# A planned order and split copies from two PSUM banks, in a kernel of banded attention and a maxout layer on one core

## The chip, the cores and the metric

The kernel runs on one core of a Trainium2 chip. The metric is the time of one execution on the device in microseconds (us). Engines: PE multiplies matrices (its weight loads are listed as PEld), DVE, ACT and POOL work elementwise, SP issues most transfers. All of them take their instructions in the order in which they are given and wait for one another by semaphores.

## The reference

Attention over 4 batches of 8 heads, 768 positions of 64 values, in which a query sees the 95 keys before it, itself, and the first 8 keys of its batch, with a bias that falls linearly with the distance; then a layer that takes the elementwise maximum of three products and multiplies it by an output matrix.

```python
    scores = scale * np.matmul(q, k.transpose(0, 1, 3, 2))
    is_global = pos[None, :] < int(n_global)
    is_local = (rel >= 0) & (rel < int(n_local))
    scores = scores + bias[None, :, :, :]
    scores = np.where(keep, scores, -1000000000.0)
    ...
    a = a / (np.sum(a, axis=-1, keepdims=True) + 1e-09)
    return np.matmul(a, v).astype(np.float32)
...
    h = np.maximum(np.maximum(x @ w1, x @ w2), x @ w3)
    return (h @ w_out).astype(np.float32)
```

x is the attention's output as 3072 rows of 512; w1, w2 and w3 are 512 by 768, w_out is 768 by 512.

## The kernel before

The 3072 rows are 24 tiles of 128, six to a batch. The second layer takes them in seven chunks of 4, 2, 2, 4, 4, 4 and 4 tiles. There is no loop over the work: a string, `SCHEDULE`, lists 494 units, and the program emits them one after the other. So the string is the order on every engine and in the SP queue. A unit is a letter and numbers; where a last number chooses an engine, 0 is ACT, 1 DVE and 2 POOL. The units:

- `l n.s`: load part s of group n of q and k (line 152, SP). The groups are 2, 2, 2, 6 and 6 tiles: tiles 0 to 17. `c n.s.how` casts it to bf16 (line 179), `x n.s.how` transposes it on PE into a PSUM tile and copies that to `qkT` (line 227). In the groups of 2 a part is all of q or all of k; in those of 6 a part is one pair of heads, 0 to 3 of q and 4 to 7 of k.
- `L`, `C`, `X`: the same for one tile (18 to 23). `X T.4` transposes by a DMA from SP (line 250). `C T.1.how` casts v of tile T; in `C T.how`, 3 means q on DVE and k on POOL (lines 195 to 197). `v T` loads v (line 170).
- `S T.g.how`: scores of tile T, four of its heads, against itself and the tile before, then the exponential on ACT (lines 268 to 289). With how 1 the bias is added by two matmuls (line 275); else `M T.g` multiplies by a mask on DVE (line 302). `K` and `B` prepare masks and bias.
- `G` and `V` carry the 8 global keys and values along (lines 210 and 219).
- `A T.how`: probabilities times v, then the normalisation on DVE (line 311: reciprocal, L331, and product, L332), which gives xb. `T T.how` transposes it into the chunk's `xT`: with 4 by a DMA from SP, else on PE with a copy (line 335).
- `F c.f.j`: product j of 3 for column block f of 6 of chunk c (line 355): four matmuls, then a copy on ACT (j = 0) or a maximum on DVE (j = 1, 2). `O c.t.how`: output product of one tile, six matmuls, a copy and a store from SP (line 385). `E` does the last chunk's four tiles (line 390).
- `w`, `o`: loads of the weights; `W g.j.how`, `Q i.how` cast them.

PSUM: `sp0` and `sp1` hold one S or A each; `psH` has three banks for F, O and some transposes; `psT` has one bank for transposes. A tile that is allocated from a full pool waits until the oldest is read. Loads of q and k rotate through six buffers (`raw`), casts through five, outputs through four (`ost`).

Of the kernel before, what the change touches and what calls it, by code (L numbers as in the profile page):

```python
# [13 lines left out]
BF16 = mybir.dt.bfloat16  # L14
# [44 lines left out]


# [1 line left out]
def kernel(  # L62
# [13 lines left out]
    nc = tc.nc  # L76
# [58 lines left out]
    raw, rawv, qb, qkT, Pt, xb = {}, {}, {}, {}, {}, {}  # L135
# [41 lines left out]
    copies = (nc.scalar.copy, nc.vector.tensor_copy, nc.gpsimd.tensor_copy)  # L177
# [49 lines left out]
    def u_x(n, s, how):  # L227
        bb, t0, sz, a, j0, jn = part(n, s)
        dst = batch_T(bb)[:, a, j0:j0 + jn, t0 * 128:(t0 + sz) * 128].rearrange("c j (i e) -> c j i e", e=sz)
        pool, tag = (psH, "h") if how in (2, 3, 5) else (psT, "tp")  # L230
        tp = pool.tile([128, sz, jn, 128], BF16, name="tpp", tag=tag)
        for e in range(sz):
            for j in range(jn):
                nc.tensor.transpose(tp[:, e, j],  # L234
                                    qb["p", n, s][:, e, 2 * j:2 * j + 2].rearrange("i h d -> i (h d)"), identb)

        src = tp.rearrange("c e j i -> c j i e")
        if how >= 4 and jn > 1:
            m = jn // 2
            nc.scalar.copy(dst[:, 0:m], src[:, 0:m])  # L240
            nc.vector.tensor_copy(dst[:, m:jn], src[:, m:jn])
# [196 lines left out]
    with tc.manual_schedule():  # L438
# [9 lines left out]
        for tvar in va_ring + va_first:  # L448
# [61 lines left out]
```

## Time and profile before

| | us |
|---|---|
| median of 4 runs (lowest to highest) | 182.62 (181.99 to 182.69) |
| the profiled execution's own time | 182.59 |
| its span, first to last instruction of the profile | 180.8 |
| HBM read and written | 25.17 MB and 6.29 MB, 174 GB/s over the span |
| first matmul (x0.0) | starts at 6.10 |
| first matmul of F0.0.0 | starts at 23.34 |
| last matmul | ends at 177.1 |
| last copy (ACT, L382) | starts at 177.75 |

The profile lists busy time of each engine and its share of the span; in the lists of waits each line names who waited, for whom, the total, the number of times and the longest. In the chain of waits each row is a start, a length and the work that set the end there, and "issue" is time in which nothing was waited for. A row of a timeline is a start, a length, the engine, the line and the operation with its tiles.

### The profile page before, as it was taken

What the parts mean: (1) busy time and instruction counts of PE and PEld (TensorE: products, weight loads), DVE (VectorE), ACT (ScalarE), POOL (GpSimd) and SP (SyncE); (2) the same over time, 40 slices, a digit from 0 to 9 for tenths busy, and PEclk for the clock granted to TensorE, in tenths of its full rate; (3) what the DMA queues carried; (4) which work ended last, traced back from release to release, by engine and by line L of the source; (5) the groups of instructions that cost most, each with busy time, mean ns of one, the idle gap of its engine ahead of it and who ended that gap; (6) DMA issues with size and microseconds to landing.
All of it is one profiled execution on the core that took longest, in us unless ns stands there. A gap on an engine that the chain in (4) does not pass through costs nothing.

```text
span 180.8 us, 3992 instructions
## 1 busy us (share of the span) xinstructions
PE 167.2 (92%) x1530; PEld 95.7 (53%) x1550; DVE 123.0 (68%) x233; ACT 108.3 (60%) x165; POOL 35.7 (20%) x68
## 2 busy tenths in 40 slices
PE   0499899999999999999999999999999999999991
PEld 0356644556876667865454554544455554444451
DVE  4457858788999988887798753966596474444610
ACT  5987987766699798595774398281717412212131
POOL 6775343223521303201130020010000000000000
PEclk9999999999999999999999999999999999999999
DMA  5999998999997899689999999996702440023015
GB/s 148 271 271 259 345 318 281 384 373 339 374 241 213 246 333 240 121 177 220 192 141 116 243 245 218 185 238 136 142 0 87 180 85 0 0 96 141 0 44 188
DMA packets 70819, 35.39 MB, mean 196 GB/s; under 512 B 53392, under 2 KB 65552, under 8 KB 70800
## 3 DMA queue, kind: packets, MB, share of 16 engines
q1 hardware_dynamic: 70656, 35.07, 79.3%
q8 instruction: 12, 0.20, 0.5%
q14 instruction: 7, 0.06, 0.1%
q10 hardware_dynamic: 144, 0.07, 0.1%
HBM read 25.17 MB, written 6.29 MB: 174 GB/s over the span
## 4 chain that ended last, share of the span: by engine, by line
PE 83%; DMA 7%; DVE 3%; SPq 2%; ACT 2%; issue 1%; ACTq 0%
PE h L361 48%; PE po L376 15%; PE sp L283 7%; PE tpp L234 4%; DMA rawp<-in_k_dram 3%; PE op L322 3%; DMA raw<-in_k_dram 3%; PE op L325 2%; PE sp L275 1%; DMA out_dram<-ost 1%; SPq L168 1%; ACT P L288 1%; PE xtp L349 1%; DVE xb L332 1%; SPq L175 1%
## 5 line engine op out<-in xcount | busy, mean ns | idle before, releaser
L361 PE MATMUL h<-xT,w 128*128 128x512 bf16 (+1 forms) x490 | 99.5, 348 | 0.8
L361 PEld LDWEIGHTS <-w 128*128 128x128 bf16 x504 | 46.9, 98 | 41.1 <-issue 0.7
L288 ACT ACTIVATE P<-sp 128x1024 bf16<-128x1024 f32 (+1 forms) x48 | 43.6, 954 | 16.7 <-PE sp L283 14.7
L366 ACT CAST h<-h 128x512 bf16<-128x512 f32 (+1 forms) x42 | 21.8, 530 | 28.7 <-PE h L361 28.2
L370 DVE TENSOR_TENSOR ht<-h,h 128x512 bf16<-128x512 bf16 (+1 forms) x42 | 25.4, 609 | 13.5 <-PE h L361 12.3
L376 PE MATMUL po<-wo,ht 128*128 128x512 bf16 (+2 forms) x150 | 33.3, 362 | 0.4
L368 DVE TENSOR_TENSOR h<-h,h 128x512 bf16<-128x512 bf16 (+1 forms) x42 | 25.1, 608 | 10.5 <-PE h L361 9.1
L307 DVE TENSOR_TENSOR P<-P,wmask 128x1024 bf16<-128x1024 bf16 x36 | 24.1, 696 | 3.2 <-ACT P L288 3.1
L376 PEld LDWEIGHTS <-ht 128*128 128x128 bf16 x156 | 14.1, 98 | 14.4
L382 ACT COPY ost<-po 128x512 f32<-128x512 f32 (+2 forms) x18 | 9.9, 558 | 17.7 <-PE po L376 14.4
L234 PE MATMUL tpp<-identb,qkp 128*128 128x128 bf16 x144 | 12.6, 240 | 6.5 <-POOL qkp L184 6.1
L332 DVE TENSOR_TENSOR xb<-op,rz 128x512 bf16<-128x512 f32 x24 | 16.6, 692 | 0.8
L283 PE MATMUL sp<-qkT 64*128 64x128 bf16 x352 | 15.5, 223 | 0.9 <-ACT qkT L240 0.7
L283 PEld LDWEIGHTS <-qkT 64*128 64x128 bf16 x352 | 10.2, 96 | 10.9 <-issue 7.8
L322 PEld LDWEIGHTS <-P 128*128 128x128 bf16 x192 | 12.7, 99 | 3.4 <-DVE P L309 0.9
L234 PEld LDWEIGHTS <-qkp 128*128 128x128 bf16 x144 | 10.1, 108 | 7.9 <-POOL qkp L184 6.3
L184 POOL CAST qkp<-rawp 128x768 bf16<-128x768 f32 (+1 forms) x11 | 10.1, 922 | 18.1 <-DMA rawp<-in_q_dram 11.7
L322 PE MATMUL op<-va,P 128*128 128x65 bf16 x160 | 12.7, 195 | 0.2 <-ACT P L288 0.2
L222 POOL COPY va<-vaf 8x260 int32<-8x260 int32 x15 | 5.9, 393 | 31.4 <-PE op L325 28.1
L243 ACT COPY qkT<-tpp 128x768 bf16<-128x768 bf16 (+1 forms) x12 | 10.0, 841 | 3.0 <-PE tpp L234 3.0
L325 PEld LDWEIGHTS <-P 128*128 128x128 bf16 x160 | 10.7, 98 | 1.4
L331 DVE RECIPROCAL rz<-op 128x8 f32<-128x8 f32 x24 | 4.9, 205 | 8.6 <-PE op L325 6.9
(61 smaller groups left out, 107.3 us busy)
## 6 DMA issues: line engine op xcount, KB each, us to landing
rawv<-in_v_dram SPq DMA_DIRECT2D x24, 256.0 KB, 5.7
out_dram<-ost SPq DMA_DIRECT2D x23, 256.0 KB, 2.4
wst<-in_moe_w_dram SPq DMA_DIRECT2D x3, 1024.0 KB, 8.9
rawp<-in_q_dram SPq DMA_DIRECT2D x8, 384.0 KB, 6.1
rawp<-in_k_dram SPq DMA_DIRECT2D x8, 384.0 KB, 6.6
rawp<-in_q_dram SPq DMA_DIRECT2D x3, 512.0 KB, 6.5
rawp<-in_k_dram SPq DMA_DIRECT2D x3, 512.0 KB, 6.7
wst<-in_moe_w_dram SPq DMA_DIRECT2D x3, 512.0 KB, 7.2
```

Source lines behind the costliest of these rows:

```text
L234: nc.tensor.transpose(tp[:, e, j], qb["p", n, s][:, e, 2 * j:2 * j + 2].rearrange("i h d -> i (h d)"), identb)
L283: nc.tensor.matmul(sp[:, hh, j2, ds], qT(T - ds, 1)[hsl, jp], qT(T, 0)[hsl, jp], start=not how, stop=True, skip_group_check=True)
L288: nc.scalar.activation(P[:, :, 0:n], sp.rearrange("p a b d n -> p (a b) d n")[:, :, 0:n], AF.Exp, bias=0.0, scale=scale)
L307: nc.vector.tensor_mul(P, P, wmask[:, g, :, 0:2])
L322: nc.tensor.matmul(o, P[:, i, 0], heads(va[T])[:, h], start=True, stop=(t == 0), skip_group_check=True)
L325: nc.tensor.matmul(o, P[:, i, 1], heads(va[T - 1])[:, h], start=False, stop=True, skip_group_check=True)
L332: nc.vector.tensor_tensor(out=x.rearrange("p (g h) d -> p g h d", g=2), in0=o4[:, :, :, 0:64], in1=rz[:, :, :, None].to_broadcast([128, 2, ...
L361: nc.tensor.matmul(ps, w123[f // 2][:, dm, j, (f % 2) * 128:(f % 2) * 128 + 128], xT[c][:, dm], start=(dm == 0), stop=(dm == 3))
L366: nc.scalar.copy(h01, ps)
L368: nc.vector.tensor_max(h01s[c, f], h01s[c, f], ps)
L370: nc.vector.tensor_max(ht[c][:, f], h01s[c, f], ps)
L376: nc.tensor.matmul(po, ht[c][:, f, tt * 128:(tt + 1) * 128], wo[:, f, cols], start=(f == 0), stop=(f == NF - 1))
```

## The change

`u_x` changes for how 4 and up, the split copies. Before, one PSUM tile held the whole part, and ACT and DVE copied half of it each. Now each half has a tile of its own: the first in `psT`, copied by ACT, the second in `psH`, copied by DVE. Before, how 5 took its tile from `psH` and how 4 from `psT`. The PE transposes are the same in number and go by halves.

The string is new throughout, with the same units in the same number. Split copies are left at x0.0 and x0.1 alone (before: eight units had how 4 or 5, of which x0.1 and x1.1 had parts that could be split). Bias matmuls (S with how 1) are seven instead of five: S0.0, S1.0 and S2.1 have them now, S2.0 no longer. T11 is now a transpose on PE (`T11.0`) where it was one by DMA. The DMA transposes X18 to X23 keep their kind; C19, C21 and C22 are cast by DVE and POOL together.

```diff
@@ the order @@
-    v0 K0 K1 K2 K3 K4 K5 B0.1 B1.2 l1.0 K6 B2.0 c0.0.2 B3.0 B4.1 B5.0 B6.0 B7.2 c0.1.1 x0.0.3 x0.1.5
-    S0.0.0 l1.1 C0.1.0 M0.0 c1.0.2 S0.1.1 G0.2 v1 c1.1.2 S1.0.0 x1.0.2 C1.1.2 l2.0 l2.1 S1.1.1 G1.2 K7
-    M0.1 M1.0 A0.0 x1.1.4 M1.1 A1.1 S2.0.1 c2.0.2 x2.0.3 S2.1.0 M2.0 v2 v3 C2.1.1 V1.2 M2.1 C3.1.1 T0.1
-    G2.2 w0.0 S3.0.1 S3.1.1 G3.0 T1.0 c2.1.2 A2.0 x2.1.0 V2.2 M3.0 M3.1 A3.1 T2.0 T3.1 w0.1 w0.2 W0.0.2
-    S4.0.0 w1.0 M4.0 S4.1.0 M4.1 F0.0.0 F0.1.0 W0.1.2 v4 v5 W0.2.0 F0.0.1 F0.1.1 w1.1 W1.0.0 w1.2 G4.2
-    S5.0.0 S5.1.0 W2.0.1 V3.2 F0.0.2 F0.1.2 C4.1.2 A4.0 C5.1.2 V4.2 F0.2.0 F0.3.0 F0.4.0 M5.0 M5.1
...
-    S7.1.0 G7.1 c4.4.1 F1.4.0 x4.0.2 F1.5.0 Q0.2 M6.0 M6.1 o2 Q2.1 S8.0.0 S8.1.0 F1.4.1 F1.5.1 F1.4.2
-    F1.5.2 o1 G8.0 x4.4.0 Q1.2 A6.0 v7 v8 M7.0 M7.1 M8.0 l4.1 l4.5 l4.2 v9 O0.0.1 C7.1.0 C8.1.0 c4.1.2
...
-    O2.0.0 v18 V15.2 A16.1 O2.1.1 F4.0.0 M17.0 v19 S19.0.0 v20 S19.1.0 C17.1.1 C18.1.2 L22 L23 F4.0.1
-    F4.0.2 V16.2 G19.1 C21.0.0 X21.4 F4.1.0 F4.2.0 M17.1 A17.0 C22.0.1 M18.0 C19.1.0 C20.1.1 F4.3.0
-    F4.4.0 S20.0.0 S20.1.0 M18.1 M19.0 M19.1 T16.4 O3.0.0 O3.1.0 A18.1 F4.1.1 M20.0 M20.1 F4.2.1 T17.4
...
-    F6.0.1 F5.5.2 F6.2.0 F6.3.0 F6.1.1 O5.0.1 F6.2.1 F6.3.1 O5.1.1 O5.2.0 O5.3.0 F6.0.2 F6.1.2 F6.4.0
-    F6.2.2 F6.3.2 F6.4.1 F6.4.2 F6.5.0 F6.5.1 F6.5.2 E
+    l1.0 l1.1 K0 B0.1 B1.1 B2.1 B3.1 K1 K2 c0.0.2 K3 K4 K5 K6 B4.1 B5.0 c0.1.1 B6.1 v0 B7.1 x0.0.4
+    x0.1.4 S0.0.1 M0.0 c1.0.1 S0.1.1 G0.0 S1.0.1 x1.0.3 S1.1.1 c1.1.2 x1.1.2 C0.1.2 v1 C1.1.2 l2.0 K7
+    M0.1 A0.0 M1.0 M1.1 G1.1 l2.1 A1.1 V1.2 S2.0.0 c2.0.1 M2.0 S2.1.1 G2.2 x2.0.3 S3.0.1 v2 C2.1.1
+    S3.1.1 T0.0 c2.1.2 v3 w0.0 M2.1 C3.1.1 A2.0 V2.2 M3.0 M3.1 w0.1 w0.2 T1.0 x2.1.0 G3.0 A3.1 T2.1 T3.1
+    W0.0.2 w1.0 S4.0.0 S4.1.0 W0.1.2 F0.0.0 F0.1.0 M4.0 F0.0.1 F0.1.1 W1.0.0 W0.2.2 F0.0.2 F0.1.2 G4.2
+    S5.0.0 S5.1.0 M4.1 M5.0 F0.2.0 V3.2 F0.3.0 v4 C4.1.1 W2.0.2 F0.4.0 F0.5.0 w1.1 W2.1.0 M5.1 W1.1.1
+    w1.2 l3.0 v5 A4.0 V4.1 W1.2.0 l3.4 c3.0.0 l3.1 l3.5 l3.2 c3.4.2 c3.1.2 c3.5.2 l3.6 l3.3 l3.7 F0.2.1
...
+    C6.1.2 o2 G6.2 S7.0.0 S7.1.0 o1 F1.4.1 G7.2 c4.0.2 c4.4.2 F1.3.2 F1.5.0 Q0.2 A6.0 F1.4.2 F1.5.1 Q2.0
+    v7 l4.1 c4.1.2 Q1.1 M7.0 F1.5.2 v8 l4.5 v9 l4.2 l4.6 l4.3 l4.7 M7.1 S8.0.0 S8.1.0 C7.1.0 x4.0.2
+    x4.4.1 C8.1.2 O0.0.1 O0.1.0 A7.0 V7.2 v10 T6.1 O0.2.1 G8.0 S9.0.0 S9.1.0 T7.1 M8.0 M8.1 c4.5.1
...
+    F2.5.0 T10.4 x4.2.3 x4.6.0 x4.3.2 F2.2.2 A11.0 x4.7.0 F2.3.2 F2.4.1 F2.5.1 S12.0.0 S12.1.0 M12.0 v13
+    v14 M12.1 G12.2 T11.0 v15 v16 F2.4.2 L18 C18.0.2 L19 C12.1.0 F2.5.2 S13.0.0 S13.1.0 F3.0.0 F3.1.0
...
+    F3.5.2 T13.4 A15.1 T14.4 G16.0 T15.4 X18.4 O2.0.1 O2.1.1 O3.0.1 C19.0.3 C17.1.2 O3.1.0 M16.0 M16.1
+    S17.0.0 S17.1.0 F4.0.0 X19.4 C20.0.1 M17.0 M17.1 F4.1.0 C21.0.3 F4.0.1 F4.0.2 S18.0.0 S18.1.0 X20.4
+    F4.2.0 F4.3.0 L22 v20 v21 V15.2 A16.0 T16.4 G18.2 V16.1 L23 F4.1.1 C18.1.0 F4.2.1 F4.3.1 F4.1.2
+    A17.0 M18.0 T17.4 F4.4.0 F4.5.0 S19.0.0 S19.1.0 G19.1 C22.0.3 C23.0.2 C19.1.0 M18.1 M19.0 X21.4
+    X22.4 F4.2.2 F4.3.2 M19.1 S20.0.0 S20.1.0 F4.4.1 F4.5.1 F4.4.2 A18.0 T18.4 G20.2 A19.1 F4.5.2 O3.2.0
...
+    F5.5.2 F6.0.0 F6.1.0 F6.2.0 F6.0.1 F6.3.0 F6.1.1 F6.2.1 F6.0.2 F6.4.0 F6.3.1 F6.1.2 F6.2.2 F6.3.2
+    O5.0.1 F6.4.1 F6.4.2 F6.5.0 F6.5.1 F6.5.2 O5.1.1 O5.2.1 O5.3.1 E
@@ u_x @@
-        pool, tag = (psH, "h") if how in (2, 3, 5) else (psT, "tp")
-        tp = pool.tile([128, sz, jn, 128], BF16, name="tpp", tag=tag)
-        for e in range(sz):
-            for j in range(jn):
-                nc.tensor.transpose(tp[:, e, j],
...
-        src = tp.rearrange("c e j i -> c j i e")
         if how >= 4 and jn > 1:
             m = jn // 2
-            nc.scalar.copy(dst[:, 0:m], src[:, 0:m])
-            nc.vector.tensor_copy(dst[:, m:jn], src[:, m:jn])
-        else:
-            copies[how % 2](dst, src)
+            halves = [(0, m, psT, "tp", nc.scalar.copy), (m, jn, psH, "h", nc.vector.tensor_copy)]
+        else:
+            pool, tag = (psH, "h") if how in (2, 3) else (psT, "tp")
+            halves = [(0, jn, pool, tag, copies[how % 2])]
+        tps = [pool.tile([128, sz, hi - lo, 128], BF16, name="tpp", tag=tag) for lo, hi, pool, tag, copy in halves]
+        for (lo, hi, pool, tag, copy), tp in zip(halves, tps):
+            for e in range(sz):
+                for j in range(lo, hi):
+                    nc.tensor.transpose(tp[:, e, j - lo],
+                                        qb["p", n, s][:, e, 2 * j:2 * j + 2].rearrange("i h d -> i (h d)"), identb)
+        for (lo, hi, pool, tag, copy), tp in zip(halves, tps):
+            copy(dst[:, lo:hi], tp.rearrange("c e j i -> c j i e"))
```

## The prediction

> **What bounds the kernel now.** First I read the table of engines: one engine is busy nearly all the time.
>
> ```profile
> PE 167.2 (92%) x1530; PEld 95.7 (53%) x1550; DVE 123.0 (68%) x233; ACT 108.3 (60%) x165; POOL 35.7 (20%) x68
> ```
>
> Then the waits of PE and of its weight loads, which hold nearly all of the idle time that a new order could remove, and the chain of work that ended last, for where the exceptions lie.
>
> ```profile
> PE tpp L234 <- POOL qkp L184: 6.1, 1, 6.1
> PE xtp L349 <- DVE xb L332: 0.7, 1, 0.7
> PE sp L283 <- ACT qkT L240: 0.7, 1, 0.7
> ```
>
> ```profile
> 13.36 1.02 ACT P L288
> 14.38 0.41 ACT wmask L300
> 14.79 0.56 ACT qkT L240
> 15.37 0.69 DVE qkT L241
> 16.07 0.12 DVE rz L331
> 16.21 0.70 DVE xb L332
> ...
> 107.08 4.84 DMA raw<-in_k_dram
> 111.94 0.04 DVE qkb L199
> 111.98 0.57 issue
> 112.55 0.42 DVE P L309
> ```
>
> There are three stages. Until 6.10 us PE has no data. From 6.10 to 23.34, where F0.0.0 starts, the chain passes through ACT and DVE: the two halves of a split copy run one after the other (L240 at 14.79, then L241 at 15.37). From 23.34 to 177.1, where the last matmul ends, it is PE's own order; then 3.7 us of output follow. PE time per unit comes from the same chain: an F unit at width 512 is 0.86 (49 matmuls in 10.74), at width 256 0.44, an O unit 1.30 (18 in 3.88), a pair S.0 and S.1 0.55, an A 0.48, a T 0.22, a bias pair inside S 0.43. Over the order of before that adds to 149.6 us from F0.0.0 on, where 153.8 passed: 4.2 us over. Of these, 1.4 us are four waits seen in the timeline of starts: A4 behind its exponentials (0.4 at 29), S6.1 behind its copies (0.2 at 48.8), F4 (0.2 at 102.3), and A18 (0.55 at 113.2). The rest is about 0.09 at each of the 21 entries into S and smaller steps.
>
> A18's wait shows the kind that the change can remove. DVE had taken the cast of L22 ahead of A18's mask, and that load landed only at 111.9:
>
> ```profile
> 111.94 0.69 DVE L199 CAST qkb<-raw 128x1024 bf16<-128x1024 f32 x1 [2.83 <-DMA raw<-in_k_dram]
> 112.55 0.42 DVE L309 TENSOR_TENSOR P<-P,wmask 128x512 bf16<-128x512 bf16 x1
> ```
>
> **The change, part by part.** All sums go against the profiled execution: 182.59 us with a span of 180.8, so 1.79 outside the span; the median of the runs is 182.62.
>
> *PE work.* F, O, A, S and x units are the same in number. Seven S units carry the bias matmuls instead of five (last digit 1: S0.0, S1.0 and S2.1 gain them, S2.0 loses them). T11 leaves the DMA queue for PE: four transposes, +0.22, with an ACT copy of 0.6 in a stretch where I count ACT full (T11, then S12 and S13's exponentials and two h copies), so F3.0.1 may wait about 0.1 for its bank. From F0.0.0 on, PE's work is 149.8 instead of 149.6.
>
> *The stage before F0.0.0.* The added bias pairs run early, where PE is slow: the pair at 9.65 took 0.54 of chain, that at 11.71 0.99, so +1.53 if nothing hides them. The first lies in the 0.7 us in which PE waited at 8.57 for L240, and is free. DVE loses the mask products M0.0 and M1.0 (0.77 and 0.96), and M2.0 stands for M2.1. The split copy now has two banks, so the DVE half no longer waits for ACT's: it waited 1.1 us in all, twice. But half of it stands in the single bank of psT, so x0.1 waits for ACT's copy of x0.0 (ACT: seven wmask 3.00 from 3.73, one bias 0.5, copy 0.58, to about 7.7, 0.2 later than x0.1 starts now). ACT gives three bias products (1.3), the v0 cast (0.6) and x1.0's copy (1.02) away; DVE takes x1.0's copy (1.2) and c1.0's cast (0.7) and five more bias products at 0.46, which fit before the landing of k at 6.77 (3.67 + 5 x 0.46 = 6.0), the last two behind it. SP: v0 (1.16 between its landing and the one before) moves behind both l1 loads, so these land near 8.6 and 10.4, and v0 at 11.6; its cast on POOL ends at 12.5, two us before A0. Everything up to w1.0 lands as now.
> Laying each engine's row end to end in the new order I get: x1.0 transposes at 11.6, x1.1 at 13.8 (now 13.68), A1 done at 15.6 (now 15.26), S2.1 behind A1's xb at 16.9, x2.0 at 17.6, S3 from 18.1, A3 at 21.0, T3 at 22.45, S4 at 23.0, F0.0.0 at 23.6. It can't be before 22.8: w0.0 lands at 21.74 and POOL's cast takes 1.04. The upper end is 25.3 (the third rival). I take 23.6, +0.25.
>
> The rate of PE in this stage: eight transposes took 1.03 until 13.68 and 0.61 at 20.04, while the granted clock reads 1.00 in all windows, so the column doesn't show it; the step lies near 15.05. The Trainium skill (TensorE: Matmul & The Clock Gate, Part 1) says that the array runs at half rate until one window of some 3.4 us was busy. Filling the wait at 8.57 with a bias pair could then bring the step to about 11.6, which by my layout puts F0.0.0 at 22.9; by the row alone it stays at 23.6, and that is the sum I use.
>
> A rule speaks against the five bias products on DVE: SBUF — State Buffer (Terms) has DVE and GpSimd lock each other out for whole instructions. The row that bears on it is POOL's own bias product, 1.25 at 3.81 and 1.72 at 6.12, the longer one beside DVE's cast of 0.69. By the rule c0.0's cast on POOL at 4.92 would be held for up to one product and hold DVE in turn for 1.03, and c0.1 would be some 0.2 late.
>
> *From F0.0.0 on.* A4 moves from 29.1 to 32.6 in PE's own time, past both exponentials that it waited for (S5's end near 30.9): -0.4. S6.1 stays at 48.0; x3.7's copy ends at about 48.0, so 0.1 of its 0.2 remains. v5 moves behind w1.1, w1.2 and l3.0, which land about 1.0 sooner (31.4, 34.1, 35.2): W1.2 on ACT ends at 35.1, F0.2.2 needs it at 35.9, cover 0.8. The Q casts: Q1 (1.45 on DVE) stands between A6's normalisation and M7; I have it from 52.75 to 54.2, and O0.0 reaches its third matmul at 54.15: 0 to 0.5 of wait, 0.1 taken. A18 goes from 109.8 to 118.7, and M18.0 now precedes L22's cast; L22 is issued behind X20 near 105 and lands near 110, the cast half on DVE comes at 114: -0.55, cover 4 us. F4 (101.6) needs T15's DMA transpose: A15 ends at 95.9, xb 0.9, issue at 97, landing 2.4 to 5.8 later (the range in the answers for xT), 99.4 to 102.8: 0 to 1.2, taken 0, since L20 and L21 have landed by then. X18 stands behind T15 on SP, lands near 102, S18 needs it at 105.1. X19 and X20 stand behind four outputs, landing by 108, needed at 113 and 115. X23 lands near 128, needed at 133.5. Two entries into S fewer: -0.2. So 149.8 + (4.2 - 1.4 - 0.2) + 0.4 (the 0.1s above and one wait as small as those of now) = 152.8, against 153.8.
>
> *The end.* O5.1 to O5.3 move from before F6.1.2 to just before E. Their copies (0.69 on DVE) and outputs (landing about 2.0 after issue) lie under E's 5.2 us of matmuls; the last copy waits for an output buffer as now (0.84). 3.7 us stay.
>
> **Sum:** 23.6 + 152.8 + 3.7 + 1.79 = 181.9 us, 0.7 below.
>
> **The rivals.**
> 1. *The waits come back elsewhere* (no change). For it: counted by the units of 4 us of PE time, with the mean durations of the rows, ACT has 1.2 and 1.5 times PE's time to do around 52 and 76, DVE 1.3 times around 52 and 136, and the three psH banks pass a late copy on to PE within three units. Against: the same counts of the old order reach 1.2 and cost only 0.2. The 1.0 us of the second stage is not gained except 0.3: 182.6.
> 2. *F0.0.0 comes earlier* because PE's half rate ends sooner, at its lower bound 22.8: 181.1. For it: the wait at 8.57 is filled. Against: DVE and ACT, not PE, are named in the chain from 13.36 to 16.9.
> 3. *The early stage gets longer* (slower). Mechanism: in the first 17 us PE's order is the bound, at half rate. Both bias pairs fall on the path (1.53), after x0.1 that starts 0.2 late behind ACT's copy and with x1.0's copy 0.2 longer on DVE (1.22) than on ACT (1.02): F0.0.0 at 25.3, and 183.6 with the gain of the second stage kept. It decides from F0.0.0 at 24.9 on (183.2). For it: A0 and A1 now come behind x1.1 and two cold bias pairs. Against: ACT gives away 2.9 us there and takes on 1.25 (x0.0 half 0.58, x1.1 whole instead of half 0.44, G0 0.23).
>
> **How the numbers follow.** What this kernel's measurement can tell from no change is about 0.3%, 0.55 us: faster is below 182.07, slower above 183.17. The forecast has 0.40, rival 1 0.24, rival 2 0.12, rival 3 0.24. The forecast's own range is 181.2 to 182.6, from 0 to 0.5 at Q1 and -0.4 to +0.5 at the start; about a quarter of it lies above 182.07 once waits that I don't see are allowed for. Faster: 0.30 + 0.12 + 0.08 (the lower part of rival 1) = 0.50; slower 0.24; the same 0.26. The range 181.0 to 183.6 takes in rivals 2 and 3 at their prices and leaves out a T15 late by its full 1.2 on top of rival 3.
>
> **What would show it.** In the profile of the changed kernel: the first L361 matmul (L362 there) between 23.2 and 24.0; no idle time of PE over 0.3 after it; no cast of a raw tile on DVE ended by a DMA after 100 us; the DVE half of the split copies not ended by ACT; c0.0's cast longer than 1.03 if the port rule holds. Wrong if F0.0.0 starts after 24.9, or if the stretch from there to the last matmul takes more than 153.5.

## The result, and the profile after

The changed kernel takes 180.93 us (median of 40 runs, 180.2 to 181.98), the kernel before 182.03 (median of 61 runs, 181.28 to 184.42). The ratio is 0.9935, 95% interval 0.9921 to 0.9949: 1.1 us or 0.65% faster. The forecast was 181.9. Executions of one kernel differ by 0.3 to 3.3 us, and the profiled one can lie anywhere among them.

| us | before | after | forecast |
|---|---|---|---|
| profiled execution | 182.59 | 180.79 | 181.9 |
| first matmul of F0.0.0 | 23.34 | 23.33 | 23.6 |
| from there to the end of the last matmul | 153.79 | 152.10 | 152.8 |
| from there to the end of the span | 3.68 | 3.59 | 3.7 |
| outside the span | 1.79 | 1.77 | 1.79 |

The profile after, its table of engines first (busy time, share of the span, instructions):

```profile
PE 165.8 (93%) x1537; PEld 95.3 (53%) x1558; DVE 125.6 (70%) x246; ACT 101.2 (57%) x158; POOL 35.7 (20%) x64
```

PE's share hardly moves (92.5% to 92.6%): its busy time falls by 1.4 us and the span by 1.8. The windows of the same profile (stretch, its length, busy time and instructions of PE, PEld, DVE, ACT and POOL, granted clock, DMA share, GB/s) put the rest into the middle stage:

```profile
0.00:23.33 23.33, 14.98 (x206) 9.53 (x207) 14.73 (x41) 16.74 (x28) 9.17 (x22) 1.00 1.07 260
23.33:175.43 152.10, 150.78 (x1333) 85.75 (x1352) 110.62 (x205) 84.19 (x130) 26.53 (x43) 1.00 0.77 188
175.43:179.00 3.57, 0.00 (x0) 0.00 (x0) 0.29 (x1) 0.27 (x1) 0.00 (x0) 1.00 0.45 154
```

PE is busy for 150.78 of 152.10 us: 1.3 us are listed as idle behind F0.0.0, in gaps of at most 0.16 us. (Before, the same stretch had 152.05 of 153.79. So only 0.4 of the 1.7 us saved was listed as idle; the rest lay within what a profile with modelled ends counts as busy. PE's rate is not the cause: the median distance between two matmuls of an F unit is 216 ns in both.) The list of PE's waits (who waited for whom, total, times, longest) says the same; its five longest are:

```profile
PE tpp L240 <- POOL qkp L184: 6.2, 1, 6.2
PE xtp L350 <- DVE xb L333: 0.8, 1, 0.8
PE tpp L240 <- ACT qkT L244: 0.5, 1, 0.5
PE sp L276 <- DVE xb L333: 0.4, 1, 0.4
PE op L323 <- ACT P L289: 0.3, 1, 0.3
```

All five are of the stage before F0.0.0. Behind it the list has only two gaps of 0.16 for which it names no releaser, at 115.75 and 128.83, and these are no waits. PE's weight loads (PEld) show the eight of F4.2.2 and F4.3.2, its matmuls only seven:

```profile
115.51 1.41 PEld L362 LDWEIGHTS <-w 128*128 128x128 bf16 x8
115.75 1.67 PE L362 MATMUL h<-xT,w 128*128 128x512 bf16 x7 [0.16 <-issue]
```

The first matmul of F4.2.2 has no record; its load starts at 115.51, and the gap is its time.

What stood at A18 in the old kernel, a DVE that waits 2.83 us for a load, is gone. DVE's timeline (start, length, engine, line, operation, and in brackets the idle time before it) now reads there:

```profile
113.70 0.69 DVE L333 TENSOR_TENSOR xb<-op,rz 128x512 bf16<-128x512 f32 x1
114.31 0.42 DVE L310 TENSOR_TENSOR P<-P,wmask 128x512 bf16<-128x512 bf16 x1
...
115.66 0.42 DVE L196 CAST qkb<-raw 128x512 bf16<-128x512 f32 x1
```

M18.0 (114.31) comes first, then the cast of L22, whose two transfers had landed at 110.65 and 111.85.

In the early stage the chain of waits no longer passes through ACT at 13.36 to 15.35 and the second half of a split copy. It runs through PE's own order, and then through the normalisations of A0 and A1 (the row at 15.42 is A1's):

```profile
13.35 0.55 PE tpp L240 x8
13.91 0.27 PE op L323 x8
...
15.42 0.70 DVE xb L333
16.12 0.05 issue
16.16 0.60 PE sp L276 x2
```

### The profile page after: what moved, and what is told of

Same layout as the page of the kernel before. It is cut to its first block, busy times and chain, and to the rows that moved or that the text cites. A ratio compares the mean times of both kernels' runs of the same rounds, so it can differ in the third digit from the quotient of the medians.

```text
span 179.0 us, 3997 instructions
## 1 busy us (share of the span) xinstructions
PE 165.8 (93%) x1537; PEld 95.3 (53%) x1558; DVE 125.6 (70%) x246; ACT 101.2 (57%) x158; POOL 35.7 (20%) x64
## 4 chain that ended last, share of the span: by engine, by line
PE 89%; ACT 3%; DVE 2%; issue 2%; DMA 1%; POOL 1%; POOLq 0%; ACTq 0%
PE h L362 52%; PE po L377 16%; PE sp L284 7%; PE tpp L240 5%; PE op L323 3%; PE op L326 2%; PE sp L276 2%; ACT wmask L301 2%; PE xtp L350 1%; DMA out_dram<-ost 1%; DVE xb L333 1%; ACT ost L383 0%; ACT vaf L190 0%; DVE rz L332 0%; ACT qkT L244 0%
## 5 line engine op out<-in xcount | busy, mean ns | idle before, releaser
L377 PE MATMUL po<-wo,ht 128*128 128x512 bf16 (+2 forms) x149 | 32.5, 362 | 0.5 <-issue 0.2
L308 DVE TENSOR_TENSOR P<-P,wmask 128x1024 bf16<-128x1024 bf16 x35 | 24.9, 731 | 5.1 <-ACT P L289 4.8
L383 ACT COPY ost<-po 128x512 f32<-128x512 f32 (+2 forms) x15 | 8.2, 554 | 25.0 <-PE po L377 24.0
L240 PE MATMUL tpp<-identb,qkp 128*128 128x128 bf16 x144 | 11.7, 232 | 6.6 <-POOL qkp L184 6.2
L184 POOL CAST qkp<-rawp 128x768 bf16<-128x768 f32 (+1 forms) x13 | 12.0, 927 | 18.1 <-DMA rawp<-in_k_dram 13.7
L383 DVE COPY ost<-po 128x512 f32<-128x512 f32 (+1 forms) x11 | 7.2, 654 | 11.3 <-PE po L377 11.1
L244 ACT COPY qkT<-tpp 128x768 bf16<-128x768 bf16 (+2 forms) x15 | 11.9, 802 | 4.7 <-PE tpp L240 4.6
L323 PEld LDWEIGHTS <-P 128*128 128x128 bf16 x192 | 12.5, 97 | 2.6 <-ACT P L289 0.4
L240 PEld LDWEIGHTS <-qkp 128*128 128x128 bf16 x144 | 9.5, 104 | 7.8 <-POOL qkp L184 6.2
L326 PEld LDWEIGHTS <-P 128*128 128x128 bf16 x160 | 10.4, 97 | 1.6
L244 DVE COPY qkT<-tpp 128x768 bf16<-128x768 bf16 (+2 forms) x9 | 8.6, 954 | 3.1 <-PE tpp L240 2.9
```

Source lines behind the costliest of these rows:

```text
L240: nc.tensor.transpose(tp[:, e, j - lo], qb["p", n, s][:, e, 2 * j:2 * j + 2].rearrange("i h d -> i (h d)"), identb)
L244: copy(dst[:, lo:hi], tp.rearrange("c e j i -> c j i e"))
L308: nc.vector.tensor_mul(P, P, wmask[:, g, :, 0:2])
L323: nc.tensor.matmul(o, P[:, i, 0], heads(va[T])[:, h], start=True, stop=(t == 0), skip_group_check=True)
L377: nc.tensor.matmul(po, ht[c][:, f, tt * 128:(tt + 1) * 128], wo[:, f, cols], start=(f == 0), stop=(f == NF - 1))
```

## The experiments

All kernels here compute the full result. The start of F0.0.0 and the stretch from there to the last matmul come from one profile of each kernel, whose own time stands beside them; medians and ratios come from repeated runs beside the kernel before.

| | median us (lowest to highest) | ratio, 95% interval | profiled us | F0.0.0 | stretch |
|---|---|---|---|---|---|
| e1: old order, two banks | 182.10 (181.49 to 183.41) | 0.9983 [0.9950, 1.0015] | 183.41 | 22.88 | 155.09 |
| e2: new order, one bank | 182.84 (181.40 to 183.33) | 1.0018 [0.9988, 1.0049] | 183.29 | 25.86 | 152.06 |
| e3: new kernel, S0.0 and S1.0 by masks | 184.13 (182.12 to 185.43) | 1.0046 [1.0005, 1.0087] | 182.30 | 24.71 | 152.22 |
| e4: old kernel, C22 behind A18 | 181.75 (181.37 to 182.62) | 0.9968 [0.9939, 0.9998] | 181.70 | 23.73 | 152.52 |
| e5: new kernel, warmed up | 180.81 (180.62 to 180.89) | 0.9928 [0.9902, 0.9954] | 180.88 | 23.39 | 152.10 |
| e6: old kernel, warmed up | 181.87 (181.51 to 183.40) | 0.9999 [0.9970, 1.0027] | 183.28 | 23.61 | 154.18 |
| e7: e2, warmed up | 182.50 (181.97 to 183.28) | 1.0014 [0.9985, 1.0042] | 182.04 | 24.58 | 152.07 |
| e8: e3, warmed up | 182.25 (180.88 to 184.09) | 0.9977 [0.9942, 1.0012] | 184.06 | 26.36 | 152.26 |
| e9: old kernel, four waits moved | 182.21 (181.84 to 182.65) | 1.0003 [0.9983, 1.0023] | 182.30 | 23.43 | 153.41 |
| e10: new kernel, T11 by DMA | 182.85 (181.88 to 185.17) | 1.0021 [0.9997, 1.0046] | 182.81 | 23.82 | 153.47 |
| e11: e5, group 2 loaded late | 185.06 (184.11 to 186.04) | 1.0145 [1.0103, 1.0188] | 185.87 | 22.17 | 158.27 |
| e12: e5, v3 before l2.1 | 181.28 (180.88 to 181.66) | 0.9939 [0.9913, 0.9965] | 181.37 | 22.80 | 153.17 |

### e1 and e2: each half of the change alone

e1 is the kernel before with the new `u_x`; e2 is the changed kernel with the old one:

```diff
 (e2)
-            halves = [(0, m, psT, "tp", nc.scalar.copy), (m, jn, psH, "h", nc.vector.tensor_copy)]
...
+        pool, tag = (psH, "h") if how in (2, 3) else (psT, "tp")
+        tp = pool.tile([128, sz, jn, 128], BF16, name="tpp", tag=tag)
...
+            nc.scalar.copy(dst[:, 0:m], src[:, 0:m])
+            nc.vector.tensor_copy(dst[:, m:jn], src[:, m:jn])
```

> The order of before, with the split copies x0.1 and x1.1 from two PSUM banks. My theory (the gain is from waits removed after F0.0.0, the banks bring nothing to the end): the DVE half of the two copies starts with ACT's half instead of 0.6 us behind it, F0.0.0 stays within 0.3 us of 23.34, ratio to before 0.998 to 1.001. Rival (the two banks bring the gain): ratio 0.993 to 0.996.

> The order of the changed kernel, with one PSUM bank for each split copy (x0.0, x0.1), so the DVE half waits for ACT's half again. My theory: the start loses at most 0.3 us, F0.0.0 at 23.3 to 23.7, ratio to before 0.993 to 0.996. Rival (the banks bring the gain): ratio 0.998 to 1.001.

e1 starts F0.0.0 0.46 us earlier than before and gains nothing that can be measured. Its list of waits shows where the start went:

```profile
PE h L361 <- DMA xT<-xb: 1.1, 1, 1.1
...
PE op L322 <- ACT P L288: 0.7, 1, 0.7
```

The second is A4 waiting for its exponentials: A4 begins at 29.57 in e1 and in the kernel before, so the 0.46 is spent there. The first is F4.0 waiting for T15's DMA transpose. PE would have come to F4.0 at 102.38, as before (102.44), but here SP issued that transpose at 99.79 instead of 98.68, because the issue of X19 ahead of it took 2.55 us (1.26 before). e6 has the same long issue (2.52) and the same wait, from a start of 23.61; what makes the issue long is not shown. The profiled execution of e1 took 183.41 where the median is 182.10, so 155.09 says little of the others.

In e2 the theory that the order brings the gain by itself fell. Its stretch is as short as the changed kernel's (152.06), so the shorter stretch is the order's; but it starts 2.5 us later. PE's timeline of e2, and then of the changed kernel, at x0.1's transposes:

```profile
8.66 1.01 PE L234 MATMUL tpp<-identb,qkp 128*128 128x128 bf16 x8 [1.52 <-DVE qkT L241]
```

```profile
6.18 1.03 PE L240 MATMUL tpp<-identb,qkp 128*128 128x128 bf16 x8 [6.18 <-POOL qkp L184]
7.68 1.01 PE L240 MATMUL tpp<-identb,qkp 128*128 128x128 bf16 x8 [0.47 <-ACT qkT L244]
...
11.75 0.84 PE L240 MATMUL tpp<-identb,qkp 128*128 128x128 bf16 x8
```

With one bank, x0.1 waits until ACT and DVE have read x0.0's tile one after the other (1.52 us); with two it waits for ACT's half alone (0.47). The new order splits two parts that follow directly on each other, so it needs the second bank. This wait is 1.05 of the 2.5 us; PE's rate also stepped up later in this execution (near 16.4, in the changed kernel near 12.2). The gain is not a sum of the two halves: neither half alone gains.

### e3: without the two early bias pairs

```diff
-    x0.1.4 S0.0.1 M0.0 c1.0.1 S0.1.1 G0.0 S1.0.1 x1.0.3
+    x0.1.4 S0.0.0 M0.0 c1.0.1 S0.1.1 G0.0 S1.0.0 x1.0.3
```

> The changed kernel with S0.0 and S1.0 masked by DVE products instead of bias matmuls. If PE's step to full rate at about 11.6 (15.05 before) came from PE being kept busy by the bias pairs, the step goes back towards 15: x1.0's eight transposes take 1.03 again, and F0.0.0 comes at 23.5 to 24.2. If the step depends on nothing in PE's order, it stays at 11.6 and F0.0.0 at 23.0 to 23.5. Time either way: ratio to before 0.993 to 0.999; each 0.1 us of F0.0.0 is 0.0005.

x1.0's transposes take 1.04 again, as expected, but the time and the start lie outside both expectations: it is slower than the kernel before, at the edge of what can be told. PE has less to do and F0.0.0 starts 1.38 us later:

```profile
11.10 1.04 PE L240 MATMUL tpp<-identb,qkp 128*128 128x128 bf16 x8 [0.46 <-DVE qkp L184]
...
15.92 0.20 PE L323 MATMUL op<-va,P 128*128 128x65 bf16 x1 [1.63 <-ACT wmask L301]
```

The wait of 1.63 is A1's. The row names ACT's mask of K7, which ended at the same time (15.88), but the changed kernel runs A1 before that mask. What A1 needs here is M1.0's mask product, which DVE runs from 15.18 to 15.86, behind A0's normalisation:

```profile
14.57 0.69 DVE L333 TENSOR_TENSOR xb<-op,rz 128x512 bf16<-128x512 f32 x1
15.18 0.68 DVE L308 TENSOR_TENSOR P<-P,wmask 128x1024 bf16<-128x1024 bf16 x1
```

S2.1, and F0.0.0 with it, come 1.4 us later than in the changed kernel, as A1 does (15.92 against 14.47). In e8 below, where the mask ended earlier, the same wait of 1.63 is put down to this product:

```profile
16.13 0.20 PE L323 MATMUL op<-va,P 128*128 128x65 bf16 x1 [1.63 <-DVE P L308]
```

So the added bias pairs are not only PE time. They take a mask product away that in this order stands behind A0's normalisation on DVE, in front of A1. The profiled execution of e3 took 182.30; nine of the twelve took 183.17 to 185.43, and of these there is no profile.

### e4 and e9: the old order, mended by hand

e4 moves one cast, C22, from before M18.0 to behind A18. e9 does that and puts an F or O unit ahead of each of A4, S6.1 and F4.0 (lines are shown in part):

```diff
 (e4)
-    M17.1 A17.0 C22.0.1 M18.0
+    M17.1 A17.0 M18.0
...
-    O3.0.0 O3.1.0 A18.1 F4.1.1
+    O3.0.0 O3.1.0 A18.1 C22.0.1 F4.1.1
 (e9, besides)
-    C4.1.2 A4.0 C5.1.2 V4.2 F0.2.0 F0.3.0
+    C4.1.2 C5.1.2 F0.2.0 A4.0 V4.2 F0.3.0
...
-    F1.3.1 S6.1.0 G6.2 S7.0.0 F1.2.2
+    F1.3.1 F1.2.2 S6.1.0 G6.2 S7.0.0
...
-    A16.1 O2.1.1 F4.0.0
+    A16.1 O2.1.1 O3.0.0 F4.0.0
...
-    T16.4 O3.0.0 O3.1.0 A18.1
+    T16.4 O3.1.0 A18.1
```

> Before with one unit moved: the cast of L22 stands behind A18 instead of ahead of A18's masks. My theory: A18's wait of 0.55 us is gone and nothing takes its place, ratio 0.996 to 0.998. Rival (the wait is taken up by later slack or comes back at X22): 0.999 to 1.001.

> Before with the four waits of the second stage covered by small moves and nothing else: F0.2.0 ahead of A4, F1.2.2 ahead of S6.1, O3.0 ahead of F4.0, the cast of L22 behind A18. The start is that of before. Theory (the steady part of the gain is these waits): from F0.0.0 to the last matmul 152.2 to 152.7 us (153.8 before, 152.1 in the changed kernel), ratio to before 0.992 to 0.996. Rival (the waits come back elsewhere): 153.3 or more, ratio 0.998 or more.

e4 does what was expected: moving one cast that waits for a load brings 0.3% (0 to 0.6%), about half of the change's gain (the intervals don't allow more than "a good part"), and its stretch is 152.52. That is 1.27 less than before, and more than A18's wait: in this execution, which reaches F0.0.0 0.39 later, A4 and F4.0 don't wait either. e9, which was to bring more, brings nothing that can be measured; its stretch is 0.38 shorter. Its timeline at A18 shows why; the rows are PE's, ACT's and PE's again:

```profile
111.25 1.47 PE L376 MATMUL po<-wo,ht 128*128 128x512 bf16 x6
111.28 1.95 ACT L288 ACTIVATE P<-sp 128x1024 bf16<-128x1024 f32 x2
...
113.28 0.42 PE L322 MATMUL op<-vaf,P 128*128 128x65 bf16 x8 [0.56 <-ACT P L288]
```

The O3.0 that e9 put ahead of F4.0 is the one that stood between S20's scores and A18. With O3.1 alone (1.30 of work from 111.25) A18 comes while ACT is still at S20's exponentials, and waits 0.56 again. A wait was moved from F4.0 to A18: filler units are a fixed stock, and each has one place. The wait named for S6.1 was not met either: by the starts of the matmuls it lies at F1.3.1 (0.15 at 48.54 before, 0.15 at 48.22 in e9), ahead of the unit that e9 moved.

### e5 to e8: the rate of PE

The unit `D` of the kernel multiplies zeros into a PSUM tile that nothing reads. Twelve of its matmuls at the head of the string keep PE busy from 1.19 to 5.3 us, in which it has no other work. e5 adds them to the changed kernel, e6 to the one before, e7 to e2 and e8 to e3:

```diff
-    l1.0 l1.1 K0 B0.1 B1.1 B2.1 B3.1 K1 K2 c0.0.2
+    D0.12 l1.0 l1.1 K0 B0.1 B1.1 B2.1 B3.1 K1 K2 c0.0.2
```

> The changed kernel with twelve 512-column matmuls of zeros on PE ahead of everything, from about 1.2 us on, while it waits for data; they add 5 us of PE work where it idles. Theory (the spread of single times and about 1 us of the start come from when PE's rate steps up): x0.0's and x0.1's transposes take 0.6 instead of 1.03, F0.0.0 at 22.4 to 22.9 (w0.0's landing and cast are the floor), single times within 0.8 us of each other instead of 1.8, ratio to before 0.986 to 0.992. Rival (the rate doesn't matter, the chain through ACT and DVE does): F0.0.0 stays at 23.3 and the ratio at 0.993 to 0.995.

> Before with the same twelve matmuls. Theory: F0.0.0 at 22.3 to 23.0, but the waits on landings after it (A4, F4, A18) grow by what the start gains, as in the run with two banks alone; single times within 0.8 us of each other; ratio to before 0.993 to 0.998, so the changed order keeps a gain of 0.005 to 0.009 over it. Rival: the change is nothing but an earlier step of the rate, and this kernel equals the changed one with the same matmuls within 0.002.

> The changed order with one PSUM bank for each split copy, and the same twelve matmuls. x0.1's transposes still wait for both copies of x0.0 (1.52 us of wait in the run without the matmuls). Theory: of what the single bank cost, the copies' wait stays and the later step of the rate goes: F0.0.0 0.3 to 1.0 us later than in the changed kernel with the matmuls, ratio to it 1.002 to 1.006. Rival (the bank cost only through the rate): equal within 0.001.

> The changed order with S0.0 and S1.0 masked by DVE products, and the same twelve matmuls. If the added bias pairs helped because they kept PE busy, they are not needed here: F0.0.0 and the time within 0.2 us (0.001) of the changed kernel with the matmuls. If they helped because they free DVE and ACT's followers, this one stays slower by 0.003 or more.

None of the four is measurably faster than its parent; e8 against e3 comes nearest, with intervals that just overlap. So the theory of e5 missed, and the rival of e6 fell: with both kernels warmed up the change still brings 0.7% (0.9928 against 0.9999; the highest time of e5, 180.89, is below the lowest of e6, 181.51). The gain is not an earlier step of PE's rate. e7 lies 0.009 above e5, more than the 0.002 to 0.006 expected, so the second bank is needed by a warm PE too. In e5 all transposes run at the full rate, from the first:

```profile
6.16 0.62 PE L240 MATMUL tpp<-identb,qkp 128*128 128x128 bf16 x8 [0.84 <-POOL qkp L184]
...
10.57 0.62 PE L240 MATMUL tpp<-identb,qkp 128*128 128x128 bf16 x8
```

x1.0 runs 1.2 us earlier than in the changed kernel, and F0.0.0 starts no earlier (23.39). PE's waits of e5 say what has taken over:

```profile
PE op L323 <- DVE va L190: 0.8, 1, 0.8
PE op L323 <- POOL va L190: 0.7, 1, 0.7
PE sp L276 <- DVE xb L333: 0.7, 1, 0.7
```

A3 waits for the cast of v3, which landed at 20.28 (in the changed kernel at 18.87, issued at the same time, near 12.5; why is open), A1 for that of v1, and S2.1 for A1's normalisation. Loads and DVE bound the start once PE is fast. What e5 may bring is steadiness: its six runs lie within 0.27 us (180.62 to 180.89), where 40 of the changed kernel spread over 1.8; but e12, warmed up too, spreads over 0.8 in twelve.

e8 shows that a warm-up alone doesn't hold. In the profiled execution (184.06, where the median is 182.25) the transposes take 0.62 and 0.61 at 6.09 and 7.70, and 1.03 again at 10.80 and 13.16. This time the granted clock (the last figure but two) shows it:

```profile
9.00:10.50 1.50, 0.99 (x16) 0.48 (x14) 0.98 (x3) 1.41 (x4) 0.03 (x1) 1.00 1.27 262
10.50:11.00 0.50, 0.20 (x3) 0.20 (x4) 0.24 (x1) 0.50 (x1) 0.50 (x1) 0.77 1.37 218
11.00:14.00 3.00, 3.00 (x27) 1.97 (x26) 1.23 (x1) 0.99 (x2) 1.89 (x3) 0.50 1.25 258
...
15.00:17.00 2.00, 0.87 (x24) 0.76 (x24) 1.33 (x4) 0.67 (x2) 0.09 (x1) 1.00 1.29 252
17.00:18.00 1.00, 0.30 (x7) 0.13 (x2) 0.97 (x3) 0.84 (x1) 0.30 (x1) 0.80 1.34 226
18.00:20.00 2.00, 2.00 (x17) 1.02 (x16) 0.96 (x2) 0.75 (x2) 0.68 (x2) 0.50 1.11 327
```

The clock falls to 0.50 near 10.8, is back at 1.00 at 15, and falls again near 17.6, behind stretches in which PE was busy about half of the time (from 15 to 17: 0.87 of 2.00). e7, profiled at 182.04, falls once, from about 11.2 to 14.6, and e6 likewise; e6 also meets F4.0's wait for T15's transpose (1.1) as e1 does. In e5 the clock stays at 1.00 to the last matmul. Where it falls, PE has little work in a stage in which it waits often; the bias pairs and the second bank both fill that stage. Five of e8's twelve executions took 180.88 to 181.26, close to e5's; none of them was profiled. If they are the ones whose rate held, which is not shown, the pairs matter most by keeping PE busy, and the mask product that they spare costs a warm PE little.

### e10: T11 by DMA again

```diff
-    v14 M12.1 G12.2 T11.0 v15 v16 F2.4.2
+    v14 M12.1 G12.2 T11.4 v15 v16 F2.4.2
```

> The changed kernel with T11 by DMA again. PE saves four transposes (0.22 us) and ACT a copy (0.6), but F3.0.0 waits for the landing: xb of A11 near 74.3 us, T11 stands behind v13 and v14 on SP, lands near 78 to 79, F3.0.0 stood at 77. Theory: a wait of 1 to 2 us ahead of F3.0.0, ratio to before 0.999 to 1.004. Rival (the DMA is hidden): 0.992 to 0.994.

As expected: the stretch is 1.4 us longer (153.47 against 152.10), and one wait accounts for it. The transpose is issued behind the loads v13 and v14 on SP, at 76.11, and F3.0.0 needs it:

```profile
76.11 1.37 SPq L341 DMA_TRANSPOSE xT<-xb  x1
```

```profile
79.90 2.75 PE L362 MATMUL h<-xT,w 128*128 128x512 bf16 x11 [1.56 <-DMA xT<-xb]
```

### e11 and e12: is there more in the start?

e11 loads group 2 behind the values and the first weights, and computes its casts, transposes and S4 among the first F units. e12 is gentler: v3's load goes ahead of l2.1, and only S4 moves behind F0.0.0:

```diff
 (e12, against e5)
-    G1.1 l2.1 A1.1
+    G1.1 A1.1
...
-    T0.0 c2.1.2 v3 w0.0
+    T0.0 v3 l2.1 w0.0
...
-    T1.0 x2.1.0 G3.0 A3.1 T2.1 T3.1
-    W0.0.2 w1.0 S4.0.0 S4.1.0 W0.1.2 F0.0.0 F0.1.0
+    T1.0 G3.0 A3.1 c2.1.2 T2.1 x2.1.0 T3.1
+    W0.0.2 w1.0 F0.0.0 S4.0.0 S4.1.0 W0.1.2 F0.1.0
```

> A version meant to beat both: the changed kernel with the warm-up matmuls and with the loads of tiles 4 and 5 (l2, 1 MB, two landings of 1.85 us) moved behind v2, v3, w0.0 and w0.1 (w0.2), their transposes and S4 behind the first F units. In the warm kernel A1 and A3 waited for the casts of v1 and v3, and DMA is full until 20 us. Theory: v3 lands near 15.5, w0.0 near 17.2, F0.0.0 at 19.0 to 21.0 in place of 23.4; later waits on landings take back 0.5 to 2 us of it; ratio to before 0.978 to 0.990. Rival (PE then waits for the same bytes later): 0.990 to 0.994.

> The changed kernel with the warm-up matmuls of e5, and v3's load issued ahead of the second part of group 2 (l2.1), so that v3 should land near 18.4 us in place of 20.28 and l2.1 near 20.3 in place of 16.5; the cast, the transposes and S4 of that part come behind A3 and F0.0.0. It tells apart what sets the start once PE keeps its full rate. Theory (v3's landing held A3 until 20.80, the weights' first part is next at 22.88): A3's wait of 0.82 goes, F0.0.0 starts at 22.8 to 23.0 in place of 23.39, the stretch stays 152.1 to 152.5 and the time is 180.2 to 180.7, ratio 0.989 to 0.993. Rival (the slack of the early landings is used up, as in e11, and S4 with group 2's late part holds the F units): F0.0.0 near 22.9, but the stretch above 152.9 and the ratio at 0.994 or over.

Both theories missed; e12 comes close to its rival (stretch above 152.9, ratio 0.9939). e11 starts F0.0.0 at 22.17 and loses 6 us behind it: S4 and S5 then come with no work between them that could cover their exponentials,

```profile
30.66 0.40 PE L284 MATMUL sp<-qkT 64*128 64x128 bf16 x8 [0.89 <-ACT P L289]
31.58 0.40 PE L284 MATMUL sp<-qkT 64*128 64x128 bf16 x8 [0.52 <-ACT P L289]
```

and behind these waits the granted clock reads 0.50 from 33.16 to 36.58, which is about 1.7 us of lost work. PE had been busy for 1.41 of the 3.41 us before. The transposes and scores of group 2, which now lie behind F0.0.0, add to the stretch as well. In e12 v3 landed at 17.01 and A3's wait of 0.82 went, but two others took its place before F0.0.0:

```profile
21.28 0.62 PE L240 MATMUL tpp<-identb,qkp 128*128 128x128 bf16 x8 [0.57 <-POOL qkp L184]
...
22.80 1.04 PE L362 MATMUL h<-xT,w 128*128 128x512 bf16 x3 [0.67 <-POOL w L428]
```

x2.1 waits for its late cast, and F0.0.0 for the cast of w0.0, which landed at 21.64. Of the 0.59 by which F0.0.0 is earlier than in e5, 0.56 is S4's pair of scores, which I hadn't counted: it now lies behind F0.0.0 and lengthens the stretch. A ratio of 0.9939 is no better than the change itself. No kernel here beats the changed one by more than can be measured.

## Why the prediction was right and wrong

**Direction and mechanism were right, the size was too small by 0.4 us and the base too high by 0.6.** Of the signs that it named, those on F0.0.0, PE's idle times, DVE's casts and the split copies came as said; c0.0's cast told nothing. On its own base the forecast said 0.7 below; measured is 1.1 (182.03 to 180.93). The base was one execution at 182.59 beside four runs with a median of 182.62; the median of 61 is 182.03. That one profiled run and four timings stood for the kernel is the first step that failed: runs of the kernel before spread over 3 us, and three of these four, the profiled one among them, lay in the upper half. Against the profiled execution the sum was 1.1 too high, by its terms:

- **The stretch: 152.8 forecast, 152.10 measured. This is the term that was mis-sized.** The step reads 149.8 + (4.2 - 1.4 - 0.2) + 0.4, a change of -1.0 with T11's +0.2 in it; measured is -1.7. Counted by the starts of PE's matmuls in both traces, its parts are these. The four named waits (A4, S6.1's at F1.3.1, F4.0, A18; 1.4) are gone, as said. The two entries into S fewer are worth 0.4 and not 0.2: each costs 0.1 ahead of its first score and 0.1 more within the scores (the 24 of S6 and S7 take 0.88 in two blocks, 0.99 in the three of the old order). T11's transposes cost 0.2, as said. The 0.4 for new small waits had no row behind it, and nothing came of it: the new order has no new wait. Four starts look 0.22 late (O0.3, F4.2.2, O4.2 and F5.4.0), but at each the weight loads show one more than the matmuls, 8 to 7 or 6 to 5, so the gap is a first matmul without a record. The remaining 0.1 are small steps. So -1.4 - 0.4 + 0.2 - 0.1 = -1.7: the step that failed is the allowance of 0.4, and the entries at half their price. That this order meets its landings with cover to spare, and not by luck of one start, is shown by e2, e3, e5, e7 and e8: from starts of 23.39 to 26.36 the stretch is 152.06 to 152.26. An earlier start was not tried with it unchanged. In the old order it is 153.8 to 155.1 (before, e1, e6) and 152.52 in e4, not in the order of the starts; it goes by which of its waits an execution meets.
- **The start: 23.6 forecast, 23.33 measured (-0.27).** The layout by rows was 0.5 to 0.7 too late between x1.1 (13.8, measured 13.29) and S2.1 (16.9, measured 16.16), and right again at T3 (22.45, measured 22.42). The step of PE's rate came near 12.2 us, close to the 11.6 estimated from the busy window of the Trainium skill (TensorE: Matmul & The Clock Gate, Part 1), and not near 15, where the old trace had it: eight transposes took 0.84 at 11.75 and 0.62 at 13.29. Yet the price that I had set on this (rival 2: F0.0.0 at 22.8) didn't come. e5, at the full rate throughout, starts at 23.39 as well, bound by v1, v3 and DVE. Part of the 23.33 is luck: e10, whose string is the same as far as T11, stepped near 13.3 and started F0.0.0 at 23.82.
- **The tail: 3.7 forecast, 3.59 measured.** O5.1 to O5.3 behind the F units cost nothing at the end.

*Rival 1*, waits that come back elsewhere: it didn't happen. e9 shows that it is a fair fear: when waits were moved by hand in the old order, A18's stayed, at 0.56.

*Rival 3*, the early stage longer by two cold bias pairs: it didn't happen in the whole change: the pairs keep PE busy where it would have waited, and spare DVE a product. A start near its 25.3 came all the same when a part is missing: 25.86 without the second bank, 24.71 without the pairs. The prediction called the pairs a cost of up to 1.53 and the banks a removal of 1.1 us of copy time; in the profiled executions each was instead a condition for the other parts.

*T11 on PE* was costed at +0.22 and 0.1 at F3.0.1. Its worth was left out: by DMA it would have cost 1.56 at F3.0.0 (e10), since in the new order the loads v13 and v14 stand before it on SP.

*The five bias products on DVE.* DVE's row and POOL's row of the changed kernel:

```profile
3.68 1.43 DVE L296 TENSOR_SCALAR bias<-rbase 128x384 bf16<-128x384 f32 x5
```

```profile
5.08 1.04 POOL L184 CAST qkp<-rawp 128x1024 bf16<-128x1024 f32 x1 [2.01 <-DMA rawp<-in_q_dram]
```

They took 0.29 each, not the 0.46 of the sum, and ended by 5.11, so that c0.0's cast (1.04, 1.03 before) hardly met one. The 0.46 was a mean of two in the old kernel, of which the second (3.95 to 4.60) ran beside POOL's own product (3.81 to 5.06). The rule of SBUF — State Buffer (Terms), by which the cast would have been held, could not be tried on it: the two instructions hardly overlapped. The old pair fits it badly, for DVE's product began and ended inside POOL's; but spans on POOL are rough.

*Landings.* l1 at 8.66 and 10.52, v0 at 11.72, w1.1 at 31.25, w1.2 at 33.95 and l3.0 at 35.12 came within 0.15 of the forecast. T15's transpose landed at 101.24, inside 99.4 to 102.8. X18 (103.22 for 102), X20 (108.65 for 108) and L22 were 0.6 to 1.9 late and X23 3.4 late (131.44 for 128); PE waited for none of them.

**The range.** Measured is 180.93, just below its lower end of 181.0. That end joined rival 2's start to the forecast stretch; no case had a stretch below 152.8, and none had a lower base. The unknown was taken to lie at the start, and it lay in the base and in an allowance that only added. The forecast's own range was summed wrongly too: from its terms it is 181.4 to 182.8 and not 181.2 to 182.6.

## What to carry to other kernels

Judge a hand-planned order by how its main stretch takes a shifted start: if the stretch keeps its length over starts 3 us apart, the order has cover for its landings. If a unit in it begins at the same time whether the start is early or late, as A4 did in the old order, speed-ups ahead of it are eaten. Don't add an allowance for waits that no row shows; bound it from zero. Take the base from many runs, and not from the one that was profiled. Before a gap as long as one instruction is called a wait, see in the weight loads whether that instruction's record is missing. Before undoing a part that looks like pure cost (a bias by matmul, a second bank), ask which engine's queue it keeps clear and which idle time it fills, and try the whole, since parts of a plan needn't gain one by one.

## What was not expected of the hardware

- PE's rate can fall back to half after a warm-up though no single idle time is over 1 us: in e8 the clock went from 1.00 to 0.50 near 10.8, when the largest idle times had been 0.79, 0.99 and 0.67 us. It fell again near 17.6, behind an idle time of 1.63. In the 3.41 us before each fall PE had been busy for 1.83 and 1.30.
- The granted clock shows such a later fall, and not the half rate at the start of a kernel that was not warmed up: in the changed kernel it reads 1.00 from the first window, while eight transposes take 1.03 at 6.18 and 0.62 at 13.29. There the duration of a repeated instruction is the better view. The trace's own record of the clock begins only at 12.25 (before: 15.08; e2: 16.35; e10: 13.27; e3: 13.30), where those durations change; the windows print 1.00 for the time without a record.
- The half-rate spells in the records have one length, 3.41 us: 11.29 to 14.71 in e6, 11.15 to 14.57 in e7, 10.77 to 14.19 and 17.60 to 21.01 in e8, 33.16 to 36.58 in e11. Counted back from the first step in such stretches, the step of the changed kernel ends the first one that PE filled (8.84 to 12.25, busy for 3.41), and so it does in e2 (12.94 to 16.35, busy for 3.41; the one before had 3.16) and in the kernel before (11.66 to 15.08). In e3 2.96 us of work were enough. So the delay between steady work and the step isn't constant: 4.6 us in the changed kernel, where PE is busy from 7.68 on, and 6.0 in e2, where it is from 10.35 on.
- A later step costs time: e10 has the string of the changed kernel as far as T11, and its step came 1.0 us later. x1.0's eight transposes took 1.03 at 11.75 (0.84), S2.1 started at 16.66 (16.16) and F0.0.0 at 23.82 (23.33). That this is what spreads the runs of one kernel over 2 to 3 us fits, but was not shown: one execution of each was profiled.
